# A rounding VectorE step in place of three, in the conversion of 64 bit weights beside an attention and a mixer on one core

## The chip, the cores and the metric

The kernel runs on 1 core of a Trainium2 chip. The metric is the device time in microseconds of one launch, as the median of several runs; lower is better. Engines are called by the names of the profile: PE (TensorE), DVE (VectorE), ACT (ScalarE), POOL (GpSimd), SP (SyncE, which issues most transfers).

## What is computed

A chunked attention (64 tokens to a chunk) feeds a low-rank mixer over the tokens and then a two-layer network over the channels. q, k and v are 32 bit floats. U, V, w_ch1 and w_ch2 arrive as 64 bit floats, since each is multiplied by a 64 bit scale when it is drawn.

```python
# B, H, S, D = 8, 8, 576, 64
q_c, k_c, v_c = (z.reshape(B, H, S // 64, 64, D) for z in (q, k, v))
scores = (1 / np.sqrt(D)) * np.matmul(q_c, k_c.transpose(0, 1, 2, 4, 3))
attn = np.exp(scores - scores.max(-1, keepdims=True))
attn = attn / (attn.sum(-1, keepdims=True) + 1e-09)
x = np.matmul(attn, v_c)             # then heads side by side: B x 576 x 512
u = x + (x.transpose(0, 2, 1) @ U @ V).transpose(0, 2, 1)     # rank 32
out = u + np.maximum(u @ w_ch1, 0.0) @ w_ch2                  # 512 -> 2048 -> 512
```

## The kernel before

**The steady work.** The 4608 tokens are taken as 4 pairs of batches (1152 tokens, 9 tiles of 128), each pair in 3 groups of 3 tiles. For each group and each of 16 slices f of the 2048 hidden channels, `hidden` (line 757, 12 matmuls) makes h, ACT makes its rounded relu `hh` (L766), DVE the remainder `hl` (L771), and `project_out` (L784, 9 matmuls) adds to the group's output banks. Every product is taken as high and low parts, so it is three matmuls. The pair (hidden and output) of one group and one slice is called a block here. 32 blocks make up the two first groups of the first pair.

**The weights.** Slice f of both weight matrices (W0 to W15, 1 MB of 64 bit words each) is loaded by SP (L327, L331) into a tile `wraw` and converted into 32 bit, then split into a high and a low part. [...]

```python
nc.scalar.activation(af, raw[..., 1].bitcast(F32), AF.Abs, scale=2.0**16)   # L99, ACT: |hi| as a float
```

then six DVE steps of `as_f32` (L103 to L115): clamp (L105), shift the exponent into place (L106), put the sign back (L109), cut out the power of two (L112), scale `lo` by it (L113), add (L114). L112 and L113 write into `hi`, that is, into the raw tile. After them ACT writes the high part (L350) and DVE the low one (L353). W0 to W12 are converted in one piece of 1024 elements to a partition, W13 to W15 in two of 512; U (320) and V (144) go the same way.

**The order of the first part.** The attention of the first pair, the weights and the first 32 blocks are written down as operations `Op(engine, us, run, *after, take, free)`. `order()` is a planner: it lets a list of operations run in simulated time with these costs, with limited buffers (`ROOM`; 16 slots `w` hold raw tiles, converted tiles and early q, k, v tiles alike) and ranks, and the program is written in the order that comes out. On the chip every engine takes its own instructions in that order, one after the other. `rounding` (L213) enters the six DVE steps with their costs. Where PE is planned to be idle, `fill` (L151) adds matmuls that compute nothing, by the planned length of the gap. From block 8 on, one transfer after each block (`halve`, L389; 288 KB in pieces of 128 bytes) re-sorts q and k of the second pair in DRAM; after blocks 25 and 27 the first two attention tiles of the second pair come in between.

**The rest.** From the third group on (some 200 us of 940), the order is a written list in the code, and no weight is converted any more.

Names in rows: `wroom` is a weight under conversion, `qkv` an early tile of q, k and v, `qkT` and `eT` are transposed tiles, `sc` scores, `mx` and `ex` the softmax, `av` attention times values, `y`, `ys` and `u` belong to the low-rank mixer, `ut`, `uth`, `utl` are the transposed mixer output and its two parts, which `hidden` reads. Tile 7 is the last attention tile of the first pair.

Of the kernel before, what the change touches and what calls it, by code (L numbers as in the profile page):

```python
# [11 lines left out]
F32 = mybir.dt.float32  # L12
F32R = mybir.dt.float32r
U32 = mybir.dt.uint32
AF = mybir.ActivationFunctionType
ALU = mybir.AluOpType
AX = mybir.AxisListType
# [5 lines left out]
def kernel(  # L23
# [11 lines left out]
    nc = tc.nc  # L35
    B, H, S, D = q.shape

    moe_U, moe_V, moe_w_ch1, moe_w_ch2 = (a.bitcast(U32) for a in (moe_U, moe_V, moe_w_ch1, moe_w_ch2))
    R = moe_V.shape[0]
# [38 lines left out]

    uwords = wpool.tile([P, 10, 2 * R], U32, tag="w", name="uraw", bufs=NF)
    nc.sync.dma_start(uwords[:, 0:4], moe_U[0 : 4 * P].rearrange("(t p) r -> p t r", p=P))  # L80
# [7 lines left out]
    warm = const.tile([P, 1], F32, name="warm")  # L88
    nc.scalar.activation(warm, ident[:, 0:1], AF.Exp)
    ust = const.tile([P, 10, 4, R], F32R, name="ust")  # L90
# [6 lines left out]
    def magnitude(raw, a):  # L97
        af = a.bitcast(F32)
        nc.scalar.activation(af, raw[..., 1].bitcast(F32), AF.Abs, scale=2.0**16)  # L99

    def as_f32(raw, a):
        hi, lo = raw[..., 1], raw[..., 0]
        af, hf = a.bitcast(F32), hi.bitcast(F32)  # L103
        return [
            lambda: nc.vector.tensor_scalar(af, af, HI_MIN, HI_MAX, op0=ALU.max, op1=ALU.min),  # L105
            lambda: nc.vector.tensor_scalar(  # L106
                a, a, 4, 1, op0=ALU.logical_shift_left, op1=ALU.logical_shift_right
            ),
            lambda: nc.vector.scalar_tensor_tensor(  # L109
                a, hi, 0x80000000, a, op0=ALU.bitwise_and, op1=ALU.bitwise_or  # L110
            ),
            lambda: nc.vector.tensor_scalar(hi, a, 0xFF800000, None, op0=ALU.bitwise_and),  # L112
            lambda: nc.vector.scalar_tensor_tensor(hf, lo, 2.0**-52, hf, op0=ALU.mult, op1=ALU.mult),  # L113
            lambda: nc.vector.tensor_add(af, af, hf),  # L114
        ]  # L115

    def wslot(shape, dtype, name):
        return wpool.tile([P, *shape], dtype, tag="w", name=name, bufs=NF)
# [91 lines left out]
    def rounding(raw, room, after, take, n):  # L210

        st = {}
        k = n / 1024  # L213

        def begin():
            st["a"] = room()
            magnitude(raw, st["a"])
            st["steps"] = as_f32(raw, st["a"])

        o = Op("ACT", 0.2 + 0.95 * k, begin, after, turn[0], take=take)  # L220
        for z in range(6):
            us = 0.15 + 0.54 * k if z in (0, 1, 3) else 0.15 + 1.07 * k
            o = Op("DVE", us, lambda z=z: st["steps"][z](), o)
            if z == 2:
                turn[0] = o
        return o, st
# [6 lines left out]
    def conversion(raw, room, high, low, after, take, free, n):  # L233
        o, st = rounding(raw, room, after, take, n)
        return splitting(st, high, low, [o], free, n)
# [4 lines left out]
    def u_ops():  # L240
# [5 lines left out]
        def room():  # L246
            st["u"] = wslot((10, R), U32, "uroom")
            return st["u"]
# [16 lines left out]

        ld = Op("POOL", 2.7, load, take="w", lat=2.0)
        o, _ = rounding(Later(lambda: st["raw"]), room, ld, "w", 10 * R)
        w = Op("ACT", 1.4, whole, o, take="w", free="w")
        h = Op("ACT", 1.8, high, w)
# [8 lines left out]
    def v_ops():  # L278
# [5 lines left out]
        def load():  # L284
            words = wslot((2 * n,), U32, "vraw")
            nc.gpsimd.dma_start(words, moe_V.rearrange("r (b c) -> (r b) c", b=4))
            st["raw"] = words.rearrange("p (r w) -> p r w", w=2)

        def room():
            st["v"] = wslot((n,), U32, "vroom")  # L290
            return st["v"]
# [13 lines left out]

        ld = Op("POOL", 0.7, load, take="w", lat=2.5)
        o, _ = rounding(Later(lambda: st["raw"]), room, ld, "w", n)
        o = Op("POOL", 2.4, spread, o, take="w", free="w w", lat=2.5)
        o = Op("ACT", 0.7, high, o)
# [12 lines left out]
    def w_ops(f, after=None):  # L322
        st = {}

        def load():
            raw = wslot((2 * DM, 2), U32, f"wraw_{f}")
            nc.sync.dma_start(  # L327
                raw[:, 0:DM].rearrange("p (cc f) w -> p cc (f w)", cc=NCC),
                moe_w_ch1[:, 2 * f * P : 2 * (f + 1) * P].rearrange("(cc p) f -> p cc f", p=P),
            )  # L330
            nc.sync.dma_start(raw[:, DM:].rearrange("p c w -> p (c w)"), moe_w_ch2[f * P : (f + 1) * P, :])  # L331
            st["raw"] = raw
# [48 lines left out]
    halves = {}  # L381
# [85 lines left out]
    def attention_ops(pr, t, *after):  # L467
# [66 lines left out]
        def exp():  # L534
            exf = flat()
            nc.scalar.activation(exf, exf, AF.Exp, scale=SCALE)  # L536

# [226 lines left out]
    def relu_high(pr, g, f, ps):  # L764
        hh = work.tile([P, GN], F32R, tag="hh", name=f"hh_{pr}_{g}_{f}", bufs=2)
        nc.scalar.activation(hh, ps[:, :GN], AF.Relu)  # L766
        return hh
# [83 lines left out]
    for item in WORK:  # L851
        rank[0] += 1
        begin = len(ops)
        z, i = item[0], int(item[1:] or 0)
# [26 lines left out]
    for g, f0, f1 in STRETCHES:  # L881
        for f in range(f0, f1):
# [3 lines left out]
            if (g, f) == (0, NF - 1):  # L886
                last = prev
# [158 lines left out]
```

## Time and profile before

| | us |
|---|---|
| three runs | 942.73, 940.80, 939.13 |
| median of the runs | 940.8 |
| profiled execution, span from first to last instruction | 937.6 |
| PE busy in it | 916.5 (98%) |
| DVE busy in it | 488.7 (52%) |
| ACT busy in it | 212.3 (23%) |

The profile gives the profiled execution by its span; what lies around the span (start and end of the launch) is not in it, and the median of the runs is 3.2 us above the span. The span falls into a head (0 to 68 us: loads, attention of the first pair, U, V, W0 and W1, mixer), a stage of blocks with the conversions of W2 to W15 beside them (68 to about 190 us), and the rest. Busy shares over the whole span mix these, so the stages are read one by one.

### The profile page before, as it was taken

To read this page: it belongs to the slowest core of one execution; us is meant where nothing else is said; L and a number is where in the kernel's file an instruction comes from. 1 tells how busy PE (TensorE), PEld (TensorE's weight loads), DVE (VectorE), ACT (ScalarE), POOL (GpSimd) and SP (SyncE) were. 2 spreads that over 40 slices of the span, in tenths; PEclk is the share of its full clock that TensorE was granted. 3 is DMA by queue.
4 is the path that set the end of the run, shared out by engine and by line. 5 is a ranking of instruction groups with operands and counts; after the bars stand their busy time and mean duration, and the time that the engine had idled before them with its cause. 6 is when DMAs were issued, how large, how long until landed. Compare 5 with 4: busy or idle time off the path is not lost.

```text
span 937.6 us, 16153 instructions
## 1 busy us (share of the span) xinstructions
PE 916.5 (98%) x6639; PEld 806.1 (86%) x6642; DVE 488.7 (52%) x922; ACT 212.3 (23%) x379; POOL 30.1 (3%) x84
## 2 busy tenths in 40 slices
PE   7789999999999999999999999999999999999998
PEld 4569999878898888888898898988889889999997
DVE  6789999975545535553434534553433643321211
ACT  5434343322211212121211221111121211111110
POOL 5510000000000000000000000000000000000000
PEclk9999999999999999999999999999999999999999
DMA  9980688546646535563543733562231512310000
GB/s 214 222 260 1 140 168 185 138 129 146 143 98 150 127 57 130 124 127 81 129 92 79 153 70 79 150 140 68 78 91 35 148 45 46 79 23 1 35 1 34
DMA packets 271449, 98.79 MB, mean 105 GB/s; under 512 B 221296, under 2 KB 257136, under 8 KB 271376
## 3 DMA queue, kind: packets, MB, share of 16 engines
q1 hardware_dynamic: 269440, 94.81, 44.5%
q0 software_dynamic: 1328, 2.80, 1.4%
q8 instruction: 52, 0.85, 0.4%
q10 hardware_dynamic: 608, 0.15, 0.1%
q14 instruction: 21, 0.17, 0.1%
HBM read 73.84 MB, written 37.75 MB: 119 GB/s over the span
## 4 chain that ended last, share of the span: by engine, by line
PE 91%; DMA 3%; DVE 3%; issue 1%; ACT 1%; SPq 0%; POOL 0%; DVEq 0%; ACTq 0%
PE h L757 43%; PE o L784 41%; DMA qkv<-in_q_dram 2%; PE av L555 2%; PE sc L507 2%; PE u L692 1%; PE y L652 1%; PE y L653 1%; DMA vall<-vroom 1%; PE y L659 1%; PE ps_fill L151 0%; DVE eT L463 0%; PE ps_qT L477 0%; DMA us<-us_3d 0%; PE ps_kT L477 0%
## 5 line engine op out<-in xcount | busy, mean ns | idle before, releaser
L757 PE MATMUL h<-uth,w 128*128 128x384 f32 x1536 | 413.5, 337 | 1.6 <-DVE ex L528 1.6
L784 PE MATMUL o<-w,hh 128*128 128x512 f32 x1152 | 346.6, 393 | 0.0
L757 PEld LDWEIGHTS h<-uth,w 128*128 128x128 f32 x1536 | 279.8, 188 | 10.6 <-issue 1.4
L757 PE MATMUL h<-utl,w 128*128 128x384 f32 x768 | 258.1, 336 | 1.3 <-DVE utl L729 1.3
L784 PEld LDWEIGHTS o<-w,hh 128*128 128x128 f32 x1152 | 213.8, 188 | 36.7
L784 PE MATMUL o<-w,hl 128*128 128x512 f32 x576 | 214.2, 396 | 0.0
L771 DVE SCALAR_TENSOR_TENSOR hl<-h,hh 128x384 fp32r<-128x384 f32 x192 | 105.5, 549 | 203.3 <-ACT hh L766 202.8
L766 ACT ACTIVATE hh<-h 128x384 fp32r<-128x384 f32 x192 | 94.4, 491 | 458.7 <-PE h L757 458.5
L757 PEld LDWEIGHTS h<-utl,w 128*128 128x128 f32 x768 | 144.1, 188 | 7.9 <-DVE utl L729 1.6
L784 PEld LDWEIGHTS o<-w,hl 128*128 128x128 f32 x576 | 107.4, 188 | 22.9
L463 DVE STREAM_TRANSPOSE uT<-us 128x512 f32<-128x512 f32 x27 | 29.6, 1097 | 50.7 <-PE h L757 26.9
L463 DVE STREAM_TRANSPOSE eT<-es 128x512 f32<-128x512 f32 x27 | 29.1, 1079 | 41.0 <-DMA es<-es_6d 9.5
L463 DVE STREAM_TRANSPOSE qT<-qn 128x512 f32<-128x512 f32 x27 | 19.1, 709 | 46.4 <-PE h L757 44.7
L536 ACT ACTIVATE ex<-ex 128x512 f32<-128x512 f32 x36 | 22.8, 634 | 72.4 <-DVE ex L528 60.2
L641 ACT CAST xh<-x 128x512 fp32r<-128x512 f32 x30 | 18.5, 618 | 69.7 <-DVE x L574 44.7
L698 DVE TENSOR_TENSOR x<-u,x 128x512 f32<-128x512 f32 x36 | 24.2, 685 | 19.2 <-PE u L692 19.0
L521 DVE TENSOR_REDUCE mx<-sc 128x4 f32<-128x256 f32 x72 | 27.9, 413 | 5.4 <-PE sc L507 5.4
L724 ACT CAST uth<-uT 128x512 fp32r<-128x512 f32 x27 | 16.7, 620 | 53.6 <-DVE uT L463 53.6
L574 DVE TENSOR_TENSOR x<-av,sm 128x256 f32<-128x256 f32 x72 | 27.2, 419 | 1.4 <-DMA out_dram<-x 0.3
L414 POOL MEMSET vn<- 128x8 f32 x27 | 3.1, 114 | 689.1 <-PE av L555 506.3
L796 DVE TENSOR_TENSOR x<-o,x 128x512 f32<-128x512 f32 x36 | 23.1, 677 | 3.6 <-PE o L784 3.6
L645 DVE TENSOR_TENSOR xl<-x,xh 128x512 fp32r<-128x512 f32 x30 | 20.6, 686 | 7.6 <-ACT xh L641 6.8
(85 smaller groups left out, 531.7 us busy)
## 6 DMA issues: line engine op xcount, KB each, us to landing
wraw<-in_moe_w_ch_dram SPq DMA_DIRECT2D x32, 512.0 KB
out_dram<-x SPq DMA_DIRECT2D x36, 256.0 KB
halfq<-in_q_dram SPq DMA_DIRECT2D x24, 288.0 KB
halfk<-in_k_dram SPq DMA_DIRECT2D x24, 288.0 KB
qn<-halfq SPq DMA_DIRECT2D x27, 256.0 KB
kn<-halfk SPq DMA_DIRECT2D x27, 256.0 KB
vn<-in_v_dram SPq DMA_DIRECT2D x108, 64.0 KB
qkv<-in_v_dram POOLq DMA_DIRECT2D x36, 64.0 KB, 7.3
```

What stands on the lines that cost most here:

```text
L463: turned = nc.vector.transpose(dst, src)
L507: nc.tensor.matmul(ps[e][cs, hp * C : (hp + 1) * C], lhsT=st["qT_"][rows, hp, cs], rhs=st["kT_"][rows, hp, cs], start=True, stop=True,)
L521: nc.vector.reduce_max(mx, st["sc"][e], axis=AX.X)
L536: nc.scalar.activation(exf, exf, AF.Exp, scale=SCALE)
L574: nc.vector.tensor_mul(by_head[:, heads(pr, t, e), :], st["av"][e][:, :, 0:D], st["sm"][:, e].unsqueeze(2).broadcast_to([P, HP, D]),)
L645: nc.vector.tensor_sub(st["l"], x_of[pr, i + 4 * e], st["h"])
L698: nc.vector.tensor_add(x, st["u"], x)
L757: o = nc.tensor.matmul(ps[:, :GN], lhsT=w[:, z, cc], rhs=u[:, cc, :], start=(n == 0), stop=(n == 3 * NCC - 1))
L766: nc.scalar.activation(hh, ps[:, :GN], AF.Relu)
L771: nc.vector.scalar_tensor_tensor(hl, ps[:, :GN], 0.0, hh, op0=ALU.max, op1=ALU.subtract)
L784: nc.tensor.matmul(acc[g, j], lhsT=h[:, js], rhs=w2[f][:, z], start=(first and i == 0), stop=(final and i == 2),)
L796: nc.vector.tensor_add(x, ps, x)
```

## The change

The low word is not scaled by a power of two that was cut out of the converted word. [...] Three DVE instructions of every conversion (L112, L113, L114) become one, the planner is told of four steps with the costs of the ones that stay, and the raw tile is no longer written.

```diff
+U16 = mybir.dt.uint16
...
     def as_f32(raw, a):
         hi, lo = raw[..., 1], raw[..., 0]
-        af, hf = a.bitcast(F32), hi.bitcast(F32)
+        af = a.bitcast(F32)
+        halves = a.bitcast(U16)
+        if len(halves.shape) == 2:
+            last = halves.rearrange("p (n w) -> p n w", w=2)[..., 0]
+        else:
+            last = halves.rearrange("p t (n w) -> p t n w", w=2)[..., 0]
         return [
...
-            lambda: nc.vector.tensor_scalar(hi, a, 0xFF800000, None, op0=ALU.bitwise_and),
-            lambda: nc.vector.scalar_tensor_tensor(hf, lo, 2.0**-52, hf, op0=ALU.mult, op1=ALU.mult),
-            lambda: nc.vector.tensor_add(af, af, hf),
+            lambda: nc.vector.scalar_tensor_tensor(last, lo, 2.0**-29, last, op0=ALU.mult, op1=ALU.add),
         ]
...
-        for z in range(6):
-            us = 0.15 + 0.54 * k if z in (0, 1, 3) else 0.15 + 1.07 * k
+        for z in range(4):
+            us = 0.15 + 0.54 * k if z < 2 else 0.15 + 1.07 * k
```

Six lines are added above the steps, so a line of the kernel before is 1 lower than in the changed one near L99, and 4 lower from L120 on.

Because the planner sees shorter conversions, it writes another order on every engine; DVE has 42 instructions fewer (two for each of 21 conversions). Three places matter below.

**ACT, at about 42 to 47 us.** `vst` is the mixer's V, `wroom_675` and `wroom_673` are W2, whose first step (L99, in the changed kernel L100) waits for W2's transfer. Before:

```order
L299 CAST vst<-vall 128x576
L99 ACTIVATE wroom_675<-wraw_562 128x1024
L499 COPY eT_5_680<-ps_eT_5_667 128x512
L536 ACTIVATE ex_8_672<-ex_8_672 128x512
L499 COPY eT_8_735<-ps_eT_8_717 128x512
```

Now:

```order
L303 CAST vst<-vall 128x576
L503 COPY eT_5_670<-ps_eT_5_641 128x512
L100 ACTIVATE wroom_673<-wraw_557 128x1024
L540 ACTIVATE ex_8_646<-ex_8_646 128x512
L503 COPY eT_8_730<-ps_eT_8_714 128x512
```

The copy of tile 5's transposed softmax now stands ahead of W2's first step; that of tile 8 still stands behind it.

**DVE, at about 63 to 69 us, the end of the head.** `wroom_511` is W1, `wroom_675` and `wroom_673` W2. `utl_0` from `ut_2` is the last operand that the first `hidden` needs. Before:

```order
L698 TENSOR_TENSOR x_2_714<-u_2_863,x_2_714 128x512
L698 TENSOR_TENSOR x_3_441<-u_3_913,x_3_441 128x512
L114 TENSOR_TENSOR wroom_511<-wroom_511,wraw_271 128x1024
L675 TENSOR_TENSOR ys_1_954<-y_1_566,ys_1_954 32x512
L105 TENSOR_SCALAR wroom_675<-wroom_675 128x1024
L106 TENSOR_SCALAR wroom_675<-wroom_675 128x1024
L729 TENSOR_TENSOR utl_0_901<-ut_2_949,uth_0_900 128x4x128
```

Now:

```order
L702 TENSOR_TENSOR x_2_698<-u_2_860,x_2_698 128x512
L733 TENSOR_TENSOR utl_0_906<-ut_1_932,uth_0_905 128x4x128
L702 TENSOR_TENSOR x_3_450<-u_3_883,x_3_450 128x512
L679 TENSOR_TENSOR ys_1_951<-y_1_554,ys_1_951 32x512
L112 TENSOR_SCALAR wroom_673<-wroom_673 128x1024
L115 SCALAR_TENSOR_TENSOR wroom_673<-wraw_557,wroom_673 128x1024
L733 TENSOR_TENSOR utl_0_906<-ut_2_946,uth_0_905 128x4x128
```

W1 is finished earlier, and between `ys_1` and the last `utl_0` stand a short and a long step of W2 where two short ones stood.

**SP, at about 100 to 165 us.** `wraw` rows in pairs are one W load, `halfq` and `halfk` rows the re-sorting transfers. Before, from the tenth W load on:

```order
L389 DMA halfq_1244<-in_q_dram 9x256x32 x2
L327 DMA wraw_1348<-in_moe_w_ch_dram 128x4x256
L331 DMA wraw_1348<-in_moe_w_ch_dram 128x1024
L389 DMA halfq_1244<-in_q_dram 9x256x32
L389 DMA halfk_1383<-in_k_dram 9x256x32
L327 DMA wraw_1417<-in_moe_w_ch_dram 128x4x256
L331 DMA wraw_1417<-in_moe_w_ch_dram 128x1024
L389 DMA halfk_1383<-in_k_dram 9x256x32 x2
```

Now, the last three W loads:

```order
L393 DMA halfk_1386<-in_k_dram 9x256x32
L331 DMA wraw_1447<-in_moe_w_ch_dram 128x4x256
L335 DMA wraw_1447<-in_moe_w_ch_dram 128x1024
L393 DMA halfk_1386<-in_k_dram 9x256x32
L331 DMA wraw_1487<-in_moe_w_ch_dram 128x4x256
L335 DMA wraw_1487<-in_moe_w_ch_dram 128x1024
L393 DMA halfk_1386<-in_k_dram 9x256x32
L331 DMA wraw_1539<-in_moe_w_ch_dram 128x4x256
L335 DMA wraw_1539<-in_moe_w_ch_dram 128x1024
L393 DMA halfq_1272<-in_q_dram 9x256x32 x4
```

Before, fifteen of the sixteen re-sorting transfers of the second pair stood before the last W load; now eight do, and eight follow it.

## Rows read from the trace of the kernel before

**Rows 1.** The page, span and part 1: busy time, share, instructions.

```profile
span 937.6 us, 16153 instructions
PE 916.5 (98%) x6639; PEld 806.1 (86%) x6642; DVE 488.7 (52%) x922; ACT 212.3 (23%) x379; POOL 30.1 (3%) x84
```

**Rows 2.** Windows: length, busy time of each engine, granted clock, DMA share, GB/s.

```profile
46.90:70.30 23.40, 20.97 (x237) 14.44 (x237) 20.52 (x47) 9.35 (x16) 2.56 (x5) 0.93 0.87 260
117.20:140.60 23.40, 23.40 (x121) 21.41 (x121) 22.75 (x28) 9.60 (x13) 0.00 (x0) 1.00 0.85 168
234.00:937.00 703.00, 699.05 (x4847) 624.82 (x4846) 295.23 (x581) 124.64 (x238) 2.48 (x22) 1.00 0.38 87
```

**Rows 3.** Waits of PE, 70 to 940 us: total, times, longest.

```profile
PE h L757 <- DVE ex L528: 1.6, 2, 1.1
PE u L692 <- DVE x L698: 0.8, 1, 0.8
```

**Rows 4.** Chain of waits near 100 and near 500 us: start, length, piece.

```profile
102.44 4.16 PE h L757 x24
...
503.10 2.10 PE h L757 x12
```

**Rows 5.** Groups by line and shape on DVE, 0 to 200 us: busy, mean ns.

```profile
L113 DVE SCALAR_TENSOR_TENSOR wraw<-wraw 128x1024 f32<-128x1024 uint32 x13 | 15.9, 1223 | 0.3
L109 DVE SCALAR_TENSOR_TENSOR wroom<-wraw,wroom 128x1024 uint32<-128x1024 uint32 x13 | 15.9, 1221 | 0.2
...
L114 DVE TENSOR_TENSOR wroom<-wroom,wraw 128x1024 f32<-128x1024 f32 x13 | 15.9, 1220 | 0.2
L112 DVE TENSOR_SCALAR wraw<-wroom 128x1024 uint32<-128x1024 uint32 x13 | 9.2, 704 | 0.3
...
L106 DVE TENSOR_SCALAR wroom<-wroom 128x1024 uint32<-128x1024 uint32 x13 | 9.0, 692 | 0.3
...
L113 DVE SCALAR_TENSOR_TENSOR wraw<-wraw 128x512 f32<-128x512 uint32 x6 | 4.2, 692 | 0.2
```

**Rows 6.** The page, part 5: a strided DVE instruction.

```profile
L463 DVE STREAM_TRANSPOSE uT<-us 128x512 f32<-128x512 f32 x27 | 29.6, 1097 | 50.7 <-PE h L757 26.9
```

**Rows 7.** Timeline of ACT at 44 us: start, length, instruction, idle before it.

```profile
44.29 1.12 ACT L99 ACTIVATE wroom<-wraw 128x1024 f32<-128x1024 f32 x1 [2.04 <-DMA wraw<-in_moe_w_ch_dram]
45.31 0.58 ACT L499 COPY eT<-ps_eT 128x512 f32<-128x512 f32 x1
```

**Rows 8.** Timeline of PE at 46 us and at 55 us.

```profile
45.99 0.81 PE L555 MATMUL av<-qkv,eT 64*64 64x65 f32 x32 [2.25 <-issue]
...
54.79 0.69 PE L507 MATMUL sc<-qkT 64*64 64x64 f32 x32
```

**Rows 9.** Windows of 2 us behind that gap; the clock stands before the last two columns.

```profile
46.00:48.00 2.00, 2.00 (x39) 1.93 (x40) 1.18 (x5) 0.69 (x2) 0.00 (x0) 0.75 1.20 199
48.00:50.00 2.00, 2.00 (x34) 1.67 (x35) 1.47 (x3) 1.49 (x3) 0.96 (x2) 0.50 1.17 201
```

**Rows 10.** Timeline of DVE at 56 us and at 65 to 68 us.

```profile
56.23 0.42 DVE L521 TENSOR_REDUCE mx<-sc 128x4 f32<-128x256 f32 x1
...
65.39 0.68 DVE L675 TENSOR_TENSOR ys<-y,ys 32x512 fp32r<-32x512 f32 x1 [0.36 <-ACT ys L674]
66.11 0.69 DVE L105 TENSOR_SCALAR wroom<-wroom 128x1024 f32<-128x1024 f32 x1
...
67.56 1.29 DVE L729 TENSOR_TENSOR utl<-ut,uth 128x512 fp32r<-128x512 f32 x2
```

**Rows 11.** Timeline of PE at 68 us: the first hidden that reads utl.

```profile
68.31 0.44 PE L757 MATMUL h<-utl,w 128*128 128x384 f32 x1 [1.26 <-DVE utl L729]
```

**Rows 12.** DMA, 94 to 167 us in 40 slices: GB/s.

```profile
GB/s 0 107 171 405 67 0 33 116 98 125 364 233 101 99 162 364 189 84 114 64 299 303 111 98 116 288 289 109 98 120 315 262 115 92 73 228 364 117 97 110
```

**Rows 13.** Waits of ACT, 68 to 180 us: total, times, longest.

```profile
ACT wroom L99 <- DMA wraw<-in_moe_w_ch_dram: 4.5, 3, 2.0
```

## The prediction

> **What bounds the kernel now.** The page comes first: PE is busy for 916.5 of 937.6 us, DVE for half of that [rows 1]. An average does not say where DVE matters, so the second view is the windows. In the blocks with conversions (117 to 141 us) PE is busy for all of 23.40 us and DVE for 22.75; after 234 us DVE is busy for 295 of 703 us and PE still for 699; in the end of the head (47 to 70 us) both have gaps, and the clock is granted at 0.93 [rows 2]. So the question for the conversion stage is which of two full engines sets the pace. The waits of PE answer it: from 70 to 940 us PE waits 1.6 us for the softmax and 0.8 us for one addition, and never for a converted weight [rows 3]. The chain agrees: 24 matmuls of hidden take 4.16 us beside a full DVE, 12 take 2.10 us at 503 us, where DVE is less than half busy [rows 4]. That is 173 and 175 ns for one. PE sets the pace in the blocks; only the head and two stalls are left to gain.
>
> **What goes and what comes.** A conversion of 1024 elements loses 704 + 1223 + 1220 ns [rows 5]. The new step is not in the trace. The nearest row is L109: same operation, same size, one operand read with the same stride from the raw tile, 1221 ns [rows 5]. What differs is a 16 bit operand and result. From below, the fast one-operand form gives 0.69 us [rows 5]; from above, the dearest strided DVE row is 1097 ns for 512 elements, so 2.2 us for 1024 [rows 6]. I take 1.22 us. A conversion then saves 1.93 us of DVE (2.46 to 0.95 at the ends). Thirteen full ones give 25 us; a long step of a half is 692 ns [rows 5], so the six halves give about 1.1 us each, 6.6; U and V about 1 us more. DVE thus loses some 33 of 489 us.
>
> **Blocks, 68 to 190 us: nothing.** 11 full conversions and the six halves run here, so some 28 us of DVE work go, but PE waits for none of it [rows 3], and its own 4.16 us pieces stay [rows 4]. The cover is PE's work itself; if it were gone, the price would be the DVE work, 28 us. Against this stands a rule. The rows show PE busy all the time and weight loading for 21.41 of 23.40 us [rows 2]. The Trainium skill, "Perfetto Trace Analysis", section "Identifying the Most-Contended Engine", calls matmul busy time a bad measure, since matmuls are pipelined, and asks to judge by weight loading instead. By that rule PE has 2 us of room in 23, and the stage could gain; by the rows the gain is 0, because the same 12 matmuls take no less time where DVE is half idle [rows 4]. I go by the rows; the other result is a rival below.
>
> **Head, 42 to 68 us: -1.4 us.** Five terms.
> 1. ACT waits 2.04 us for W2's transfer with the copy of tile 5's softmax behind it, which comes at 45.31 us [rows 7]; PE waits 2.25 us for that copy and then runs its 0.81 us of attention times values [rows 8]. Now the copy stands first. The product of 0.8 us then fits into the gap, unless tile 5's v lands only then: -0.7 (0 to -0.8). Late next is tile 8's softmax, still behind W2.
> 2. After that gap the granted clock fell: 0.75 in 46 to 48 us and 0.50 in 48 to 50 [rows 9]. PE was busy for both windows, so 0.25 x 2 + 0.50 x 2 = 1.5 us were lost. With the product and three fill matmuls inside the gap, I expect the clock to stay: -1.5 (0 to -1.5).
> 3. One product for `y` now stands ahead of tile 7's scores instead of behind: +1.0.
> 4. Tile 7's scores end at about 55.4 us, but its maximum starts at 56.23, behind W1 and `ys` [rows 8, 10]. In the new order `ys` is done by then: -0.75 (0 to -0.8).
> 5. Between `ys_1` and the last `utl` stood two short steps (65.39 + 0.68 to 67.56 us, 1.5 us) [rows 10]; now a short and a long one (0.69 + 1.22): +0.5. W1's long step ahead of `ys_1` is gone too, but `ys_1` waited for PE there.
>
> The sum is -1.45, taken as -1.4. The first `hidden`, which read `utl` at 68.31 after 1.26 us of waiting [rows 11], would do so at about 66.9. Bounds: without the second term it is 0, without the second and the fourth +0.8; with no cost from the third, -2.4.
>
> **The two stalls of the first attention tiles, near 183 and 193 us: -0.4 us.** They are 1.1 and 0.5 us, PE waiting until the softmax has freed a bank [rows 3]. The first is scores, maximum and subtraction in a row, and stays. Before the second, DVE was working off conversions; these are over by then now. I take 0.4 of its 0.5 us (0 to -1.6, both).
>
> **Queues.** POOL's order does not change. SP has the W loads earlier and half of the re-sorting transfers after them; that is the third rival. The planned fills are 40 in place of 42; they run in gaps and cost nothing while the gaps stay.
>
> **Sum.** 937.6 - 1.4 - 0.4 = 935.8 us of span. The median of the runs was 3.2 us above the profiled span; with the same distance 939.0 us. That is 0.2% less, below the half per cent (4.7 us) that a measurement of this kernel tells from no change.
>
> **Rivals.**
> - *The head gains nothing* (chance 0.20): W2 or tile 5's v lands later and the clock falls as before. For it: the transfers decide when anything there starts [rows 7]. Against it: the copy no longer waits for W2. Time: 939.0 + 1.4 = 940.4.
> - *DVE was the bound of the blocks* (0.04), the result that the skill's rule leads to. With PE's room of 2 us in 23.4 [rows 2] over 120 us, the stage would lose up to 10 us: 929. For it: DVE is 97% busy. Against it: no wait of PE names a weight [rows 3], and the pace is that of the later stage [rows 4].
> - *W loads come late and hold up ACT* (0.13), slower. The conversions are planned earlier, so W10 to W15 are loaded within some 7 blocks, 7 x 8.3 / 2 = 29 us, between re-sorting transfers. In the row of rates a W load shows as a peak near 364 GB/s, 1.05 MB in 2.9 us, and a re-sorting transfer of 288 KB as a stretch near 100 GB/s, 2.9 us [rows 12]. Six of one and seven of the other are 38 us, 9 us more than there is. ACT takes its queue in order, so a first conversion step that waits for its W keeps `hh`, and PE's output matmuls, behind it. Before, ACT waited 4.5 us in three such waits, the longest 2.0, and PE felt none [rows 13, 3]. The point where it decides: a W more than about 2 us later than the `hh` behind it. Price: 9 - 2 = 7 us at worst, in the middle 5: 944. Against it: part of the 38 us overlaps, and only waits with an `hh` behind them count.
> - *The new step does not do what it says* (0.03): 16 bit stores in strides are dear. At the upper bound of 2.2 us the third place of the head grows by 1 us, 940. It would decide in the blocks only where a weight's work exceeds two blocks, 8.3 us: 0.69 + 0.69 + 1.22 + 1.22 for the steps that stay and 1.1 for two `hl` leave 3.4 us for it.
>
> **How the numbers follow.** The forecast has 0.60, at 939.0 with its bounds from 936 to 941. Runs before spread from 939.13 to 942.73, so a median moves by 1.5 us on its own. The range of 935.3 to 943.8 takes in the first rival and the smaller half of the third. Faster by over 0.5% (below 936.1): the DVE rival (0.04) and the end of the forecast where all the head's terms and both stalls fall together, 0.09; 0.13 in all. Slower by over 0.5% (above 945.5): the upper half of the third rival, 0.06, and 0.01 for the rest; 0.07. The same: 0.80.
>
> **What would show it.** Right: the new step at 1.2 us; DVE busy at about 456 us; the 24-matmul pieces still at 4.16 us; the first `hidden` reading `utl` at about 67 us; no half clock after 46 us. Wrong: a shorter piece per block (then DVE was the bound); PE waiting for ACT's `hh` between 100 and 150 us with ACT waiting for `wraw` ahead of it (third rival); the gap at 44 us as long as before (first rival).

## The result, and the profile after

| | before | changed |
|---|---|---|
| median | 941.85 us (6 runs, 939.13 to 943.17) | 946.3 us (6 runs, 945.59 to 948.48) |
| profiled execution, span | 937.6 us | 943.8 us |
| ratio of the runs, 95% interval | | 1.0058, 1.0039 to 1.0078 |

The change makes the kernel slower by 0.6%, some 5 us (4.5 us by the medians). The forecast was 939.0 us, no change; its range ended at 943.8. A second measurement of the changed kernel, beside other runs, gave 1.0054 (1.0033 to 1.0075).

The step itself does what was expected. The page's first rows, and the groups of the two long steps (busy, mean ns of one), changed kernel:

```profile
span 943.8 us, 16117 instructions
PE 919.6 (97%) x6636; PEld 807.9 (86%) x6640; DVE 458.9 (49%) x880; ACT 211.3 (22%) x379; POOL 30.4 (3%) x84
```

```profile
L118 DVE SCALAR_TENSOR_TENSOR wroom<-wraw,wroom 128x1024 uint16<-128x1024 uint32 x13 | 17.7, 1362 | 0.3
L115 DVE SCALAR_TENSOR_TENSOR wroom<-wraw,wroom 128x1024 uint32<-128x1024 uint32 x13 | 15.9, 1222 | 0.2
L118 DVE SCALAR_TENSOR_TENSOR wroom<-wraw,wroom 128x512 uint16<-128x512 uint32 x6 | 4.5, 752 | 0.2
```

DVE is busy 29.8 us less than in [rows 1], and yet the span is 6.2 us longer for the same matmuls. Following the two executions by the same instructions tells where: the first `hidden` that reads `utl` starts at 68.89 instead of 68.31 us, the first output product at 75.49 instead of 73.29 (+2.2); the first `hidden` of the third group at 215.27 instead of 210.65 (+4.6); the last output products that follow a `hidden` at 935.50 instead of 929.36 (+6.1). So 2.2 us are lost by 75 us, 2.4 between there and 211, and 1.5 over the rest.

**The first place, 67 to 75 us.** The timeline of PE (the wait in brackets; [rows 11] is its row of before), then windows of 1 us, the granted clock ahead of the last two columns:

```profile
68.89 0.45 PE L761 MATMUL h<-utl,w 128*128 128x384 f32 x1 [1.80 <-DVE utl L733]
...
75.49 0.62 PE L788 MATMUL o<-w,hh 128*128 128x512 f32 x2
```

```profile
70.00:71.00 1.00, 1.00 (x6) 1.00 (x5) 1.00 (x3) 0.00 (x0) 0.00 (x0) 0.55 0.00 0
...
73.00:74.00 1.00, 1.00 (x7) 1.00 (x6) 0.69 (x1) 0.73 (x2) 0.00 (x0) 0.74 0.00 0
```

The wait is 0.54 us longer than before, as the short and the long step of W2 ahead of `utl` predicted. Then the granted clock falls to 0.50, the lower of its two levels, for about 3.5 us, and the same matmuls from `utl` to the first output product take 6.60 in place of 4.98 us: 1.6 more.

**The second place, near 130 us.** Waits of PE, 70 to 300 us ([rows 3] of before has neither `hh` nor `hl`), and of ACT, 70 to 170 us:

```profile
PE o L788 <- DVE hl L775: 2.2, 2, 1.4
PE u L696 <- DVE x L702: 0.8, 1, 0.8
PE o L788 <- ACT hh L770: 0.7, 1, 0.7
```

```profile
ACT wroom L100 <- DMA wraw<-in_moe_w_ch_dram: 11.4, 4, 4.8
```

ACT's wait was 4.5 us in three [rows 13]; now it is 11.4 in four. The timelines of ACT, DVE and PE show how the longest gets to PE:

```profile
128.90 1.12 ACT L100 ACTIVATE wroom<-wraw 128x1024 f32<-128x1024 f32 x1 [4.85 <-DMA wraw<-in_moe_w_ch_dram]
129.93 0.47 ACT L770 ACTIVATE hh<-h 128x384 fp32r<-128x384 f32 x1
```

```profile
130.05 0.69 DVE L111 TENSOR_SCALAR wroom<-wroom 128x1024 f32<-128x1024 f32 x1 [3.59 <-ACT wroom L100]
130.66 0.55 DVE L775 SCALAR_TENSOR_TENSOR hl<-h,hh 128x384 fp32r<-128x384 f32 x1
131.36 1.23 DVE L357 TENSOR_TENSOR w<-wroom,w 128x1024 fp32r<-128x1024 f32 x1 [0.15 <-ACT w L354]
132.51 0.69 DVE L112 TENSOR_SCALAR wroom<-wroom 128x1024 uint32<-128x1024 uint32 x1
133.23 1.22 DVE L115 SCALAR_TENSOR_TENSOR wroom<-wraw,wroom 128x1024 uint32<-128x1024 uint32 x1
134.37 0.55 DVE L775 SCALAR_TENSOR_TENSOR hl<-h,hh 128x384 fp32r<-128x384 f32 x1
```

```profile
130.45 0.74 PE L788 MATMUL o<-w,hh 128*128 128x512 f32 x2 [0.66 <-ACT hh L770]
134.97 0.50 PE L788 MATMUL o<-w,hl 128*128 128x512 f32 x1 [1.37 <-DVE hl L775]
```

W12's first step stands on ACT ahead of `hh` of block (1, 6) and waits for its load; on DVE the next three instructions of conversions, late for the same reason, stand ahead of `hl` of block (0, 7). PE waits 0.66 and 1.37 us. Why the load is late shows in SP's timeline (start, length of the issue, transfer):

```profile
121.05 3.01 SPq L331 DMA_DIRECT2D wraw<-in_moe_w_ch_dram  x1
124.12 0.48 SPq L335 DMA_DIRECT2D wraw<-in_moe_w_ch_dram  x1
124.71 0.79 SPq L393 DMA_DIRECT2D halfk<-in_k_dram  x1
...
138.85 2.53 SPq L331 DMA_DIRECT2D wraw<-in_moe_w_ch_dram  x1
141.43 0.49 SPq L335 DMA_DIRECT2D wraw<-in_moe_w_ch_dram  x1
142.01 11.41 SPq L393 DMA_DIRECT2D halfq<-in_q_dram  x4
155.54 11.71 SPq L393 DMA_DIRECT2D halfk<-in_k_dram  x4
167.31 2.94 SPq L421 DMA_DIRECT2D qn<-halfq  x1
```

Eight re-sorting transfers (halvings, below) in a row take 25.3 us up to the next row, 3.2 us each. Some of them also wait for their block; g4's sixteen, below, do not, and take 3.0 us each. From 106.13 to 138.85 us SP starts five loads and six halvings in 32.7 us, so a load has (32.7 - 6 x 3.2) / 5 = 2.7 us, or 2.9 with 3.0 for a halving: the two kinds follow one another and hardly overlap. Two windows show it, the first with two halvings under way, the second with W12's load; the last two columns are the busy share of the DMA engines and GB/s:

```profile
120.00:124.00 4.00, 4.00 (x23) 3.75 (x22) 3.97 (x5) 2.16 (x3) 0.00 (x0) 1.00 0.88 100
126.00:128.00 2.00, 2.00 (x11) 1.70 (x10) 0.46 (x1) 0.00 (x0) 0.00 (x0) 1.00 1.05 382
```

The code charges the queue 0.6 us for a halving. So with short conversions the planner's own list has the load of W12 14.5 us behind the first halving; on the chip it starts 18.3 us behind it (102.73 and 121.05 us). The Trainium skill, "DMA: Bandwidth & Descriptors", section "Specifications", asks for at least 512 bytes in a piece for full rate. The rows fit that: 288 KB in pieces of 128 bytes take 3.0 to 3.2 us, as long as a load of 1 MB. The two also differ in where they write (DRAM, and the tile `wraw`), and no run here separates that from the size of the pieces.

The halvings hold up the loads in a second way. Each waits for its block, and SP, which takes its queue in order, waits with it. SP's waits, 95 to 175 us, then its timeline in g4, where no halving stands ahead of the load of W10:

```profile
SPq L393 <- PE h L761: 23.3, 4, 15.1
```

```profile
91.89 0.37 SPq L333 DMA_DIRECT2D wraw<-in_moe_w_ch_dram  x1
```

The longest of these waits, 15.1 us, ends at 102.7 us with the first halving; the load of W10 is behind it and starts at 106.13 us in place of g4's 91.89. How much of the lateness each of the two ways makes, no run tells.

### The profile page after: what moved, and what is told of

Same layout as the page of the kernel before. It is cut to its first block, busy times and chain, and to the rows that moved or that the text cites. A ratio compares the mean times of both kernels' runs of the same rounds, so it can differ in the third digit from the quotient of the medians.

```text
span 943.8 us, 16117 instructions
## 1 busy us (share of the span) xinstructions
PE 919.6 (97%) x6636; PEld 807.9 (86%) x6640; DVE 458.9 (49%) x880; ACT 211.3 (22%) x379; POOL 30.4 (3%) x84
## 4 chain that ended last, share of the span: by engine, by line
PE 90%; DMA 3%; DVE 3%; SPq 1%; issue 1%; ACT 1%; ACTq 0%
PE h L761 41%; PE o L788 40%; PE av L559 2%; PE sc L511 2%; DMA qkv<-in_k_dram 1%; DMA qkv<-in_q_dram 1%; PE u L696 1%; PE y L656 1%; DMA us<-us_3d 1%; PE y L663 1%; PE y L657 1%; DMA us_3d<-x 1%; SPq L442 0%; PE ut L708 0%; PE ps_qT L481 0%
```

## Experiments

Ratios are to the kernel before, measured beside it on the same chip, with 95% intervals.

**The step or the order (e1, e2).** e1, from the changed kernel, tells the planner of the six old costs, two of them for steps that issue nothing; e2, from the kernel before, tells it of four, and the last issues three old steps.

```diff
 e1, from the changed kernel
-        for z in range(4):
-            us = 0.15 + 0.54 * k if z < 2 else 0.15 + 1.07 * k
+        for z in range(6):
+            us = 0.15 + 0.54 * k if z in (0, 1, 3) else 0.15 + 1.07 * k
...
+            lambda: None,
+            lambda: None,
             lambda: nc.vector.scalar_tensor_tensor(last, lo, 2.0**-29, last, op0=ALU.mult, op1=ALU.add),
```

> The new single step with the order of work of the kernel before: the planner is given the six old costs per conversion, two of them for steps that issue nothing, so that PE, ACT, POOL and SP hold the rows of the kernel before and VectorE the same rows less 42. Theory A (the loss comes from the order that the planner writes from four costs, at two places: 2.2 us up to 75 us, 2.2 us near 130 us): none of it is there, 938 to 942 us, ratio to before 0.997 to 1.001, first reading of the last utl at 68.3 us or earlier. Theory B (the step itself is to blame: 1.36 us and strided 16 bit halves in place of 1.22 us of whole words, slower for whoever waits on a conversion): 945 to 947 us, as the changed kernel.

> The six old steps in the order of the changed kernel: the planner is given four costs, and the fourth entry issues the last three old steps one after the other. PE, ACT, POOL and SP hold the rows of the changed kernel. Theory A (order): as slow as the changed kernel or slower, 946 to 951 us, since the old steps add 1.8 us to a full conversion ahead of the same waiting rows. Theory B (step): 940 to 943 us, as the kernel before.

e1: 1.0012 (0.9999 to 1.0025), 941.86 us; e2: 1.0284 (1.0269 to 1.0300), 967.79 us. The new step costs nothing that can be told in the old order, and its interval lies below the changed kernel's. The old steps are far worse in the new order than expected. Windows of e2 (PE, PEld, DVE first), and its waits, 70 to 210 us:

```profile
75.00:100.00 25.00, 20.80 (x105) 18.12 (x103) 24.59 (x29) 9.46 (x14) 0.00 (x0) 0.98 0.25 85
100.00:125.00 25.00, 22.62 (x96) 19.55 (x97) 24.23 (x30) 9.56 (x13) 0.00 (x0) 0.88 0.37 73
```

```profile
PE o L784 <- DVE hl L771: 14.2, 10, 3.4
```

DVE is full and PE waits ten times for `hl`: an order made for short conversions packs them so closely that DVE becomes the bound when they are long. The loss belongs to the order, not to the step.

**Head and loads apart (e3, e4).** The planner is given four costs up to W2 and six from W3 on (e3), or the reverse (e4, with `is False`). Where it is given six, the last two are for steps that issue nothing.

```diff
+        new = (rank[0] <= WORK.index("W2") + 1) is True
+        for z in range(4 if new else 6):
...
+            o = Op("DVE", us, lambda z=z: st["steps"][z]() if z < 4 else None, o)
```

> The new step everywhere; the planner is given four costs for U, V, W0, W1 and W2 and the six old ones from W3 on, so that VectorE's rows are those of the changed kernel up to the first hl of the second group (about 72 us) and the later loads of W are spread as before. Theory A: only the head's part of the loss remains, first reading of the last utl near 68.9 us, half clock at 70 to 73.5 us, no wait of PE for hh near 130 us: 942.5 to 945 us. If the loads of W alone cost: 940 to 942 us. If the head alone: 945 to 947 us.

> The new step everywhere; the planner is given the six old costs for U, V, W0, W1 and W2 and four from W3 on, so that the head's rows are those of the kernel before and the loads of W come as close together as in the changed kernel. Theory A: only the loads' part of the loss remains: last utl read at 68.3 us or earlier at full clock, PE waits 1.5 to 2.5 us for hh and hl between 120 and 140 us: 942.5 to 945 us. If the head alone costs: 940 to 942 us. If the loads alone: 945 to 947 us.

Both missed: 1.0101 (1.0078 to 1.0125) and 1.0113 (1.0100 to 1.0127). Up to 180 us they split as expected. Waits of PE, e3 at 56 to 170 us and e4 at 70 to 210 us:

```profile
PE h L762 <- DVE utl L734: 1.8, 1, 1.8
```

```profile
PE o L789 <- ACT hh L771: 1.6, 2, 1.0
```

e3 has the first place and no wait for `hh`, e4 the second only (1.0 us at 133 us; the other 0.6 comes at 208 us). But both mixed orders meet a new wait at the second attention tile, near 212 us, 5.0 us in e3 and in e4

```profile
PE av L560 <- DVE eT L468: 4.0, 1, 4.0
```

with 7 us at half clock beside it, which costs more than either place. A half-changed list of costs gives a third order, not half of a change. The next runs leave the planner alone.

**Single rows moved in the changed order (f1 to f4).** After planning, f1 moves two rows on DVE, f2 one on ACT and three on DVE, f3 all of them; f4 keeps the order and adds matmuls in PE's wait. `behind` moves the operations that its second argument picks right behind the last one that its third picks; `utl` are the two `utl` operations that follow W2's steps.

```diff
 f1
+        plan = behind(plan, lambda o: o.item == "W2" and o.step in (1, 2), lambda o: o in utl)
 f2
+        plan = behind(plan, lambda o: o.item == "W12" and o.step == "m", lambda o: o.eng == "ACT" and o.key == (0, 7))
+        plan = behind(plan, lambda o: o.item == "W12" and o.step in (0, 1, 2), lambda o: o.eng == "DVE" and o.key == (0, 7))
 f4
+        for _ in range(8 if (pr, g, f) == (0, 0, 0) else 0):
+            nc.tensor.matmul(ps[:, :GN], lhsT=w[:, 0, 0], rhs=uh[:, 0, :], start=True, stop=True)
```

> The changed kernel with two rows moved on VectorE alone: the two steps of W2's conversion (0.69 and 1.22 us) that stand between ys and the last utl go behind it and the utl that follows. PE, ACT, POOL and SP keep the changed kernel's order. Theory A (head: this order makes PE wait 1.8 us, and the wait brings half the clock at 70 to 73.5 us): PE reads the last utl about 1.2 us earlier, near 67.6 us, the clock stays full up to 75 us, in all 2 to 3 us less than the changed kernel: 943 to 945 us. Rival (the head's lag is not on the path, or the half clock comes anyway): 946 to 947 us.

> The changed kernel with W12's magnitude on ScalarE moved behind hh of block (0, 7), and W12's first three steps on VectorE behind hl of that block; all else in the changed kernel's order. Theory A (the load of W12 comes later than the planner thought, and what waits for it stands ahead of hh and hl in the queues): PE's waits of 0.7 and 1.4 us near 130 us go, 943.5 to 945 us. Rival (the wait moves to the next block, since conversions are short of time there): 946 to 947 us with waits of the same sum between 130 and 160 us.

> Both edits of the two runs ahead together. Theory A: the two savings add, 940.5 to 943 us, so that the changed kernel's step is as fast as the kernel before in its own order but for two places. If both places share one cause and only one pays: 943.5 to 945 us.

> The changed kernel in its own order, with eight extra matmuls on PE (128x384, 0.17 us apart, into the bank that the first hidden product overwrites) while it waits for the last utl at 67.1 to 68.9 us. The wait itself stays. Theory A2 (of the head's 2.2 us, some 1.6 are the half clock that follows PE's idle time): the last utl is still read at 68.9 us, the clock stays full from 70 to 73.5 us, 944 to 945.3 us. Rival (the half clock follows something else, or costs nothing that lasts): 946 to 947 us.

| | ratio | median |
|---|---|---|
| f1 | 1.0032 (1.0019 to 1.0046) | 944.44 us |
| f2 | 1.0025 (1.0009 to 1.0040) | 943.38 us |
| f3 | 1.0013 (0.9996 to 1.0030) | 942.41 us |
| f4 | 1.0043 (1.0026 to 1.0060) | 945.80 us |

f3 lies clear of the changed kernel's interval and cannot be told from before: six moved rows take back some 4 of the 5 us. f1 is in its range, f2 0.1 us below it; f4 is 0.5 us above, between its two theories. The intervals of f1, f2 and f4 still touch the changed kernel's, so each one's share is less sure than the sum. In f2 the rival is half right: steps of W12 and W13 now stand ahead of a later block's `hl`, and of the two waits of 2.0 us one of 1.5 is left, at 138 us (in f3 too, at 135 us). In f4 the timeline of PE shows what was meant: the matmuls fill the wait, and the clock stays full up to 75 us. That the matmuls kept it there is not shown, since it stays full in a2, below, without them.

```profile
65.44 1.56 PE L760 MATMUL h<-uth,w 128*128 128x384 f32 x8
66.84 0.34 PE L763 MATMUL h<-uth,w 128*128 128x384 f32 x1
67.58 0.44 PE L763 MATMUL h<-utl,w 128*128 128x384 f32 x1 [0.40 <-DVE utl L733]
```

**The cause of the late loads, and better versions (g1, g2, g4, a2).** g1 is e1 with `utl` first, g2 is f1 with the halving's measured price in the planner, g4 puts all halvings behind the loads, a2 is the changed kernel again.

```diff
 g2, from f1
-                Op("SP", 0.6, second.pop(0), prev[0], lat=3.0)
+                Op("SP", 3.2, second.pop(0), prev[0], lat=3.0)
 g4, from the changed kernel
-                Op("SP", 0.6, second.pop(0), prev[0], lat=3.0)
+                Op("SP", 0.6, second.pop(0), prev[0], lat=3.0).key = "halving"
...
+        plan = behind(plan, lambda o: o.key == "halving", lambda o: o.eng == "SP" and o.item == "W15")
```

> The new step in the order of the kernel before (as in e1), with two of W2's short steps (0.69 us each) moved on VectorE behind the last utl and the one after it. If the 1.3 us for which PE waits there in the kernel before and in e1 are on the path, as the runs so far say: 1.2 to 1.5 us less than e1, 939.5 to 941 us, ratio to before 0.997 to 1.000. Rival (what is won there is lost again at the next wait, the first attention tiles): 941.5 to 942.5 us.

> As f1 (the changed kernel, utl first), and the planner charges the SP queue 3.2 us for a halving in place of 0.6 us: what one takes of the queue when eight follow each other (eight in 25.3 us between 142.0 and 167.3 us). Its four costs per conversion stay. Theory A (the loss near 130 us comes from a plan in which loads of W land earlier than the queue can deliver them): the planner now puts W12's magnitude behind hh of block (0, 9) by itself, no wait of PE for hh or hl over 0.5 us between 120 and 170 us, 941 to 943 us, as f3. Rival (a planned order of this kind is luck, another wait of 1 to 4 us comes up elsewhere): 943.5 to 947 us.

> The changed kernel with the 16 halvings moved on SP behind the last load of W, all other rows as in the changed kernel. Theory A (halvings of some 3.2 us each on the queue hold up the loads of W): W12's magnitude no longer waits 4.9 us, PE has no wait for hh or hl between 120 and 140 us; the halvings, 16 times 3.2 us after the last load, then end at 172 to 180 us instead of 167.3 us, so that the first qT may make PE wait by up to 3 us at 182 us: 943.5 to 946 us. Rival (the loads wait for room that conversions free, not for the queue): the waits near 130 us stay as they are, and the halvings end later: 946 to 950 us.

> The changed kernel once more, on the same chip as the other three. 945.5 to 948 us by the run shown; the waits at 67 and 130 us and the half clock at 70 us come again if they belong to the order. After 200 us, where orders are alike and the first profile lost 1.5 us more: if that is chance of single executions it differs by about a microsecond here, if it belongs to the order it is the same 1.5 us at the same places.

g2: 0.9988 (0.9974 to 1.0002), 941.21 us, clear of f1. One number in the planner, with f1's two rows, does at least what six moved rows did: W12's first step goes behind `hh` of block (0, 9), and PE has no wait for `hh` or `hl` from 70 to 210 us. g1: 0.9991 (0.9975 to 1.0008), 941.04 us. Both beat the changed kernel by 0.6% and can't be told from the kernel before.

g4: 1.0130 (1.0107 to 1.0152), 955.02 us. The mechanism is confirmed, though g4 takes away both of its ways at once, and the price was missed. ACT no longer waits for any load between 70 and 170 us and the waits near 130 are gone, but the halvings end late, and PE pays for it once:

```profile
133.96 11.36 SPq L395 DMA_DIRECT2D halfq<-in_q_dram  x4
...
170.31 12.31 SPq L395 DMA_DIRECT2D halfk<-in_k_dram  x4
182.67 2.94 SPq L423 DMA_DIRECT2D qn<-halfq  x1
```

```profile
PE o L791 <- DVE hl L778: 11.4, 1, 11.4
```

The sixteen took 48.7 us, 3.0 each; I had put their end at 172 to 180 us. The first `qT` then waits on DVE with an `hl` behind it. Loads and halvings share the transfers' time, and either can be the late one.

a2: 1.0054, 946.87 us, as expected. Both waits come again, at the same places (1.8 us for `utl`; 0.9 and 1.4 us near 127 and 131 us). The half clock at 70 us does not. Its timeline of PE:

```profile
67.36 0.44 PE L761 MATMUL h<-utl,w 128*128 128x384 f32 x1 [1.80 <-DVE utl L733]
...
72.36 0.63 PE L788 MATMUL o<-w,hh 128*128 128x512 f32 x2
```

That is 5.00 us from `utl` to the first output product, as before the change. This profiled execution is the fastest of a2's ten (943.28 us); how often the half clock comes in the others is not on record.

**More fills in the head (h1, h2).** Since stretches of half clock come in every execution's head, g1 and g2 were given more filling matmuls there (1.6 in place of 0.7 times the planned gap).

> g1 with more of the kernel's own filling matmuls on PE: in each planned gap of the first 50 us 1.6 times the gap's length over 0.23 us in place of 0.7 times, 53 more in all, no other row changed. Theory A3 (the stretches at half clock that the head shows in every execution, at 12 and at 32 or 47 us, follow PE's waits for q and k and cost some 1.6 us each): the stretch at 32 or 47 us is gone, and perhaps that at 12 us, 1.5 to 3 us less than g1, 938 to 940 us. Rival (the fills only stand in the way of a transpose that is ready): as g1 or up to 2 us more, 941 to 943 us.

> g2 with the same, 52 more filling matmuls. Theory A3: the stretch at 45 us, 6.5 us long in g2's profile, goes or is shorter, 1.5 to 3 us less than g2, 938 to 940 us. Rival: as g2 or up to 2 us more, 941 to 943 us.

A miss: 1.0024 (1.0013 to 1.0034) and 1.0050 (1.0037 to 1.0062), 3 and 5 us more than without. The stretch at 12 us is gone in both, but one at 32 us (h1) or 48 us (h2) stays, and the fills stand in the way: in h1, 43 run up to 12.85 us, when q had arrived by 12.23 us in g1, and the first `hidden` starts at 69.48 instead of 66.37 us.

## Why the prediction was wrong

- **The new step, 1.22 us:** measured 1.36 us, 0.14 more, inside its bounds. DVE busy 458.9 us; about 456 was forecast. Right, and not the reason (e1).
- **Blocks, 0:** right that nothing is gained. From 150 to 175 us DVE is busy for 8.9 of 25 us only, and the 24-matmul piece still takes 4.16 us as in [rows 4] (a window, PE, PEld and DVE first, and a piece of the chain of waits):

```profile
150.00:175.00 25.00, 25.00 (x128) 22.73 (x128) 8.91 (x17) 4.47 (x9) 0.11 (x1) 1.00 0.74 108
```

```profile
153.43 4.16 PE h L761 x24
```

  So the share of weight loading, one of the two measures that the Trainium skill, "Perfetto Trace Analysis", section "Identifying the Most-Contended Engine", asks for, would have misled here, and the second rival falls. Wrong in the sentence that the cover is PE's work itself: what PE needs from ACT and DVE is also a matter of what stands ahead of it in their queues.
- **Head, -1.4:** this step failed. At its own place, the first `hidden` that reads `utl`, it measured +0.6, and +2.2 at the first output product. The first term came: PE's wait for the copy at 44 us is 0.48 instead of 2.25 us. The second did not: the half clock after 46 us is gone, but a stretch at 32.5 to 36 us took its place, and e1, in the old order, shows it there too. It was no property of the order to be gained, and the two stretches of before are two again up to 50 us. The fourth did not come either: `ys` is done, but a short step of a conversion took its place ahead of tile 7's maximum, which starts 0.86 us after the scores end. The rows are PE's wait, the scores, that step and the maximum:

```profile
44.50 0.84 PE L559 MATMUL av<-qkv,eT 64*64 64x65 f32 x32 [0.48 <-ACT eT L503]
...
55.09 0.69 PE L511 MATMUL sc<-qkT 64*64 64x64 f32 x32
```

```profile
55.92 0.69 DVE L111 TENSOR_SCALAR wroom<-wroom 128x1024 f32<-128x1024 f32 x1
56.64 0.42 DVE L525 TENSOR_REDUCE mx<-sc 128x4 f32<-128x256 f32 x1
```

  With the third term, which cannot be read off alone, the sum up to the first `hidden` is 0 (66.75 against 66.71 us). The fifth was right (+0.54 for +0.5), but the prediction stopped at the wait: it did not price the half clock that may follow a wait that grows from 1.26 to 1.8 us.
- **Two stalls, -0.4:** near the number by luck. From 175 to 205 us PE waits 1.7 us in place of 2.4. Both waits for the softmax shrink, from 1.1 and 0.6 to 0.2 us in all, though the first was to stay; and a new one of 0.8 us comes at 183 us, for an `hl` that stands on DVE behind the first `qT`.
- **Third rival, 0.13:** this is what happened, at the place, with the sign and by the chain of waits that it named. Its transfers were priced well (2.9 us each; 2.7 to 2.9 for a load and 3.0 to 3.2 for a halving measured). The argument that held its chance down, that part of the 38 us overlaps, was the wrong one: they follow one another. Its price was too high, 2.0 to 2.4 us for a middle of 5, because only one of ACT's four waits had something behind it that PE lacked.
- **The rest, 1.5 us:** not forecast, and it need not be the order's. After 214 us PE loses 0.5 to 3.4 us against the profiled execution of before in every kernel traced, in single waits of 0.2 to 1.2 us: 1.7 in a2 and e1, 0.5 in g1, and e1 and g1 have the old order. That execution of before was a fast one: a run's time lies 1.7 to 2.3 us above its span wherever both are on record, so a span of 937.6 us belongs to a run of some 939.5 us, 2 us under the median of 941.85. The changed kernel's profiled run took 945.76 us, 0.5 under its median. So the two spans differ by 6.2 us, and the medians by 4.5. The order's share in the rest stays open.

The sum had 935.8 us of span and it came to 943.8: 3.6 from the head (-1.4 forecast, +2.2 measured), 2.8 from 75 to 211 us (-0.4 and +2.4; the two waits near 130 us are 2.0 of it), and 1.5 from the rest; 0.1 is rounding. The median then lies 2.5 us above the span, where the forecast took 3.2.

## What to carry to other kernels

When a planner writes the order, a changed cost is a changed order on every engine, and a saving that nothing waits for can only be lost there: try the new instructions in the old order first. A cheaper step makes the plan ask more of what it shares with others; here the transfers became the pace, and the planner charged the queue a fifth of one's price. With queues taken in order, look at what stands behind an instruction that waits for a transfer.

## What the runs showed of the hardware

- The same PE wait of 1.8 us ahead of `utl` was followed by 3.5 us at half clock in the changed kernel, f2, e2 and e3, and not in a2 and g4; waits of 1.3 us and less there (before, e1, e4, f1, f3, f4, g1, g2) never were. Each such stretch costs 1.6 us (6.60 us in the changed kernel and 6.55 in f2 against 4.98 to 5.04 us in before, a2, g4 and f4, for the same matmuls). The Trainium skill, "TensorE: Matmul & The Clock Gate", section "What's actually happening", says that PE's activity is looked at in windows that run freely and do not start with the kernel. The rows fit that: one and the same wait costs or doesn't.
- The step that reads and writes every second 16 bit integer takes 1362 ns where the 32 bit one of the same operation takes 1222, 11% more for half of the bytes written.
